# A gated linear recurrence and a ReGLU layer in one kernel: steps 0 and 1 regrouped from two batches of 128 tokens a unit to one batch of 256

## The chip, the cores and the metric

The kernel runs on one core of a Trainium2 chip. The metric is the device time of one execution in microseconds; the figure compared is the median of several executions. The profile and the trace are of one execution, whose own time is given beside its span.

## What is computed

```python
B, H, S, D = 4, 8, 768, 48                    # q, k, v, f_logit: [B, H, S, D], float32
f = 1.0 / (1.0 + np.exp(-f_logit))
for t in range(S):
    state = f[:, :, t, :, None] * state + np.einsum('bhd,bhe->bhde', k[:, :, t], v[:, :, t])
    y[:, :, t] = np.einsum('bhd,bhde->bhe', q[:, :, t], state)
x = y.transpose(0, 2, 1, 3).reshape(B * S, H * D)          # 3072 x 384
out = (np.maximum(x @ w_gate, 0) * (x @ w_val)) @ w_out    # weights 384x1536, 384x1536, 1536x384
```

The kernel works in bf16 inside; inputs and outputs are float32.

## The kernel before

**Chunks and steps.** The recurrence is cut into chunks of 128 tokens. Step c (0 to 5) handles chunk c of all four batches, 512 tokens, and then the feed-forward layer of those 512 tokens. Inside a chunk the recurrence becomes matmuls: the logarithm of the gates is summed over tokens (cum, L567 and L568, or L715), its exponentials scale k and q ("hats", L579 and L583, or L737 and L740), the hats are transposed so that the head dimension lies on partitions (qkT), k times q gives scores (L618 or L780), a causal mask multiplies them (ptm, L623 or L785), and scores times v (intra, L646 or L807) plus q times the state at the chunk's start (inter, L636, the first rounds of L807, or L813) gives x. The state is k hats times v (L684 or L841) added to the old state and scaled by the chunk's decay (L540, L544, L546).

**Duos, in steps 0 and 1.** `attention_duo` takes two batches at once. Batch 2·pr lies on partitions 0 to 63 and batch 2·pr+1 on 64 to 127, and each partition holds two neighbouring tokens, so that a row in memory is 384 bytes long. `load_duo` issues two transfers for each of f, k, q and v, one for each half of the partitions (L454). Even and odd tokens are handled as i = 0 and 1; `tokens` reads them back interleaved, so that x comes out in the order of the tokens. Step 0 has no state to start from, so its inter part is left out, and its state work is planned late (priority P + 30).

**Steps 2 to 5.** `attention_front` and `attention` take one batch and 128 tokens at a time, one token a partition, rows of 192 bytes (loads L466). The hats are transposed in one of two ways: on PE (L751) with a copy by DVE (L756) where the step is in `pe_hats`, which is step 2, otherwise by a transposing DMA that SP issues (L759). In steps 3 to 5 x goes through a transposing DMA too (L832).

**Feed-forward.** `ffn_hidden` makes a block of 128 hidden units: three matmuls with wg (L865), relu on ACT (L871), three with wv (L865), the product on DVE (L875). The first blocks of steps 0 and 1 are made for two batches at a time (256 columns), the others for four (512 columns). `ffn_out` multiplies by wo (L888), ACT copies the result (L898), SP stores it (L902), 192 KB a batch.

**Loads and weights.** The list `first` gives the order of the first loads and weight pieces. SP issues the loads. POOL issues the weights (L486), which are cast from float32 to bf16 on the way, in three pieces each of wg, wv and wo. "wg0@q0.1" means that wg0 is issued only after the load q0.1 has landed. Later loads wait for the landing of the load three before them (`flight`).

**The order of the work.** A planner (`Plan.listed`) sets the order ahead of time: each operation has an assumed length, the operations that it depends on and a priority, and at each step the planner takes the operation that can start first; among equals the lowest priority number goes first. Feed-forward matmuls have 1000 added, so attention goes ahead of them where both are ready. Each engine then runs its list strictly in order, with waits where an operation needs another engine's. The planner also models the two kinds of DMA (`Rings`). PE starts with filler matmuls on zeros (L936, L945) in the gaps that the planner expects before 17 us. Work on PE, DVE, ACT, POOL and SP's DMA issues is all placed this way, so that a changed length or priority can move the rest.

## Time and profile before

| what | value |
|---|---|
| median of 3 runs | 213.52 us (213.44 to 215.12) |
| the profiled execution's own time | 214.66 us |
| its span, first to last instruction | 212.9 us |
| mean granted clock of TensorE | 0.984 of full speed |
| busy: PE, DVE, ACT, POOL | 193.7, 108.6, 108.7, 81.5 us |
| feed-forward matmuls, busy: L865, L888 | 119.9 (wv 61.1, wg 58.8) and 51.3 us |
| DMA | 31.76 MB, mean 149 GB/s |
| first L865 matmul that waits for wv | 24.05 us |
| last load of step 5 issued | 141.2 us |

"Busy" of PE counts pipelined matmuls by modelled ends, so a busy PE is not a PE at its peak; start-to-start distances are the better length of a matmul. In the lines of the timeline the bracket at the end gives the idle time of the engine before the instruction and what ended it. SPq and POOLq stand for the queues that issue DMAs. A wait is put down to the releaser that came last.

### The profile page before, as it was taken

To read this page: it belongs to the slowest core of one execution; us is meant where nothing else is said; L and a number is where in the kernel's file an instruction comes from. 1 tells how busy PE (TensorE), PEld (TensorE's weight loads), DVE (VectorE), ACT (ScalarE), POOL (GpSimd) and SP (SyncE) were. 2 spreads that over 40 slices of the span, in tenths; PEclk is the share of its full clock that TensorE was granted. 3 is DMA by queue.
4 is the path that set the end of the run, shared out by engine and by line. 5 is a ranking of instruction groups with operands and counts; after the bars stand their busy time and mean duration, and the time that the engine had idled before them with its cause. 6 is when DMAs were issued, how large, how long until landed. Compare 5 with 4: busy or idle time off the path is not lost.

```text
span 212.9 us, 4759 instructions
## 1 busy us (share of the span) xinstructions
PE 193.7 (91%) x1929; PEld 109.7 (51%) x1949; DVE 108.6 (51%) x184; ACT 108.7 (51%) x235; POOL 81.5 (38%) x121
## 2 busy tenths in 40 slices
PE   7788599999998999997878999688999999999994
PEld 2265375466776764553433555253555444445562
DVE  7975564582189795664534473253533333233310
ACT  2663167444885878784372654644243344433411
POOL 8939217431795957774515453044000000000000
PEclk9999799999999999999996999999999999999999
DMA  5999999995899899996898995899222100011012
GB/s 125 242 236 220 225 205 220 216 237 121 178 237 210 179 188 189 167 226 133 191 183 183 203 221 125 150 223 150 61 50 64 37 37 37 37 39 38 37 39 109
DMA packets 108069, 31.76 MB, mean 149 GB/s; under 512 B 101136, under 2 KB 108048, under 8 KB 108048
## 3 DMA queue, kind: packets, MB, share of 16 engines
q1 hardware_dynamic: 104064, 27.93, 62.4%
q0 software_dynamic: 3984, 3.54, 10.1%
q8 instruction: 15, 0.25, 0.5%
q14 instruction: 6, 0.05, 0.1%
HBM read 25.95 MB, written 4.72 MB: 144 GB/s over the span
## 4 chain that ended last, share of the span: by engine, by line
PE 66%; DMA 18%; SPq 8%; ACT 2%; POOL 2%; issue 2%; DVE 1%
PE ps L865 37%; PE ps L888 18%; DMA qkT<-hats 5%; DMA wv<-in_moe_w_val_dram 4%; SPq L454 3%; DMA xT<-xn 3%; SPq L832 2%; DMA q_in<-in_q_dram 2%; SPq L759 2%; DMA k_in<-in_k_dram 2%; DMA f_in<-in_f_logit_dram 2%; PE ps L780 2%; PE ps L618 1%; PE ps L715 1%; PE ps L646 1%
## 5 line engine op out<-in xcount | busy, mean ns | idle before, releaser
L875 DVE TENSOR_TENSOR gT<-relu,ps 128x512 bf16<-128x512 bf16 (+1 forms) x82 | 50.2, 620 | 57.9 <-PE ps L865 51.1
L871 ACT ACTIVATE relu<-ps 128x512 bf16<-128x512 f32 (+1 forms) x82 | 44.5, 545 | 37.5 <-PE ps L865 34.3
L865 PE MATMUL ps<-xT,wv 128*128 128x512 bf16 (+1 forms) x243 | 61.1, 361 | 2.3 <-DMA wv<-in_moe_w_val_dram 2.2
L865 PE MATMUL ps<-xT,wg 128*128 128x512 bf16 (+1 forms) x231 | 58.8, 360 | 1.4 <-DMA wg<-in_moe_w_gate_dram 0.4
L888 PE MATMUL ps<-wo,gT 128*128 128x384 bf16 x288 | 51.3, 326 | 0.0
L888 PEld LDWEIGHTS ps<-wo,gT 128*128 128x128 bf16 x288 | 27.1, 98 | 19.2 <-issue 0.2
L865 PEld LDWEIGHTS ps<-xT,wv 128*128 128x128 bf16 x246 | 23.5, 100 | 24.0 <-DMA wv<-in_moe_w_val_dram 2.5
L865 PEld LDWEIGHTS ps<-xT,wg 128*128 128x128 bf16 x246 | 23.1, 100 | 20.4 <-issue 0.8
L898 ACT ACTIVATE osb<-ps 128x384 f32<-128x384 f32 x24 | 11.7, 489 | 34.3 <-PE ps L888 34.2
L785 DVE TENSOR_TENSOR ptm<-ps,tri 128x512 bf16<-128x512 f32 x32 | 21.0, 686 | 13.6 <-PE ps L780 13.5
L737 POOL TENSOR_TENSOR hats<-k_in,expo 128x384 bf16<-128x384 f32 x16 | 15.9, 999 | 22.3 <-DMA k_in<-in_k_dram 14.8
L546 POOL TENSOR_TENSOR st<-ssum,dec 128x384 bf16<-128x384 f32 x16 | 13.2, 828 | 14.1 <-DVE ssum L544 14.1
L740 POOL TENSOR_TENSOR hats<-q_in,expo 128x384 bf16<-128x384 f32 x16 | 15.9, 997 | 4.1 <-DMA q_in<-in_q_dram 4.1
L780 PE MATMUL ps<-qkT 48*128 48x128 bf16 x128 | 6.4, 219 | 6.9 <-DMA qkT<-hats 6.9
L544 DVE TENSOR_TENSOR ssum<-ps,st 128x384 f32<-128x384 f32 x16 | 8.8, 553 | 4.9 <-PE ps L841 4.7
L623 DVE TENSOR_TENSOR ptm<-ps,seen 128x512 bf16<-128x512 f32 x16 | 10.1, 685 | 2.2 <-PE ps L618 2.2
L605 DVE COPY qkT<-ps 128x1024 bf16<-128x1024 bf16 x7 | 4.8, 691 | 10.8 <-PE ps L598 10.7
L945 PE MATMUL ps<-zeros 128*128 128x512 bf16 x30 | 10.0, 481 | 0.1
L706 ACT ACTIVATE f_in<-f_in 128x768 f32<-128x768 f32 x8 | 6.7, 840 | 6.3 <-DMA f_in<-in_f_logit_dram 6.3
L772 POOL CAST vpad<-v_in 128x384 bf16<-128x384 f32 x16 | 7.9, 504 | 4.7 <-DMA v_in<-in_v_dram 4.6
L780 PEld LDWEIGHTS ps<-qkT 48*128 48x128 bf16 x128 | 3.6, 94 | 11.8 <-DMA qkT<-hats 9.5
L725 ACT ACTIVATE expo<-ps 128x384 f32<-128x384 f32 x16 | 7.9, 493 | 2.6 <-PE ps L718 2.5
(90 smaller groups left out, 182.1 us busy)
## 6 DMA issues: line engine op xcount, KB each, us to landing
out_dram<-osb SPq DMA_DIRECT2D x24, 192.0 KB, 2.2
f_in<-in_f_logit_dram SPq DMA_DIRECT2D x8, 384.0 KB, 4.7
k_in<-in_k_dram SPq DMA_DIRECT2D x8, 384.0 KB, 4.5
q_in<-in_q_dram SPq DMA_DIRECT2D x8, 384.0 KB, 5.5
v_in<-in_v_dram SPq DMA_DIRECT2D x8, 384.0 KB, 5.8
f_in<-in_f_logit_dram SPq DMA_DIRECT2D x8, 192.0 KB, 5.0
k_in<-in_k_dram SPq DMA_DIRECT2D x8, 192.0 KB, 6.5
q_in<-in_q_dram SPq DMA_DIRECT2D x8, 192.0 KB, 6.3
```

Of the source, the lines that this page charges most:

```text
L546: add("POOL", lambda: gp.tensor_tensor(t4(s_new), t4(tmp), rate, ALU.mult), [key] + dk, [f"S{b}_{c % 2}"], prio=P + 8, **pool_t(HD))
L623: last_mask[0] = add("DVE", lambda i=i, j=j, s=sj[j]: ve.tensor_tensor(ptm_all[:, m0 + i, j, :, :], s.ap[:, :].rearrange("p (n t) -> p n t ...
L737: add("POOL", lambda: gp.tensor_tensor(hk, kin[:, b % 2, :, :], ex[:, 1, :].rearrange("p (h d) -> p h d", h=H), ALU.mult), in_keys("k", c, ...
L740: add("POOL", lambda: gp.tensor_tensor(hq, qin[:, b % 2, :, :], ex[:, 0, :].rearrange("p (h d) -> p h d", h=H), ALU.mult), in_keys("q", c, ...
L780: mm = te.matmul(s.ap[:, p * C:(p + 1) * C], tokens(c, b, 1, p, lo, lo + D), tokens(c, b, 0, p, lo, lo + D))
L785: add("DVE", lambda j=j, s=s: ve.tensor_tensor(ptm[mi][:, j, :, :], s.ap[:, :].rearrange("p (n t) -> p n t", n=NP), mask, ALU.mult), [s, " ...
L865: mm = te.matmul(bank.ap[:, 0:n], wt[:, kt, j * 128:(j + 1) * 128], xT[xi][:, kt, n0:n1], start=(kt == 0), stop=(kt == NK - 1))
L871: add("ACT", lambda: sc.activation(relu[ri][:, 0:n], gate.ap[:, 0:n], AF.Relu), [gate], [f"relu{ri}"], prio=P, **act_t(n))
L875: add("DVE", lambda: ve.tensor_tensor(gT[gi][:, j, n0:n1], relu[ri][:, 0:n], val.ap[:, 0:n], ALU.mult), [val, f"relu{ri}"], [f"gT{gi}_{j}_ ...
L888: mm = te.matmul(o[b].ap[:, 0:DM], gT[gi][:, j, b * C:(b + 1) * C], wo[:, j, :], start=(j == 0), stop=(j == NJ - 1))
L898: add("ACT", lambda b=b, oi=oi: sc.activation(osb[oi][:, :], o[b].ap[:, 0:DM], AF.Copy), [o[b]], [f"osb{oi}"], prio=P, **act_t(DM))
L945: return te.matmul(spare[:, 0:WARM], zeros[:, 0:128], zeros[:, 0:WARM], start=True, stop=True, skip_group_check=True)
```

## The change

The first two steps are handled in units of one batch and 256 tokens. Unit b takes chunks 0 and 1 of batch b; units 0 and 1 give the 512 tokens of the first feed-forward step, units 2 and 3 those of the second. One transfer fills all 128 partitions, two neighbouring tokens a partition as before, so that partitions 0 to 63 hold chunk 0 and 64 to 127 hold chunk 1. The scores, the masks and x stay in the order even tokens, odd tokens, and only the store puts the rows back in place. Chunk 1 needs the state after chunk 0 of the same unit, so the decay, the state and its scaling come ahead of the scores in each unit, and an inter part follows the intra part of chunk 1. The split of a few products and copies among DVE, ACT and POOL changes. Step 2's hats are transposed by DMA like those of steps 3 to 5. The list of loads and weights has a new order and other anchors.

```diff
-    duos = (0, 1)
-    pe_hats = {2}
+    units = (0, 1)
+    pe_hats = set()
...
-    first = ("f0.0 k0.0 q0.0 f0.1 k0.1 q0.1 v0.0 v0.1 wg0@q0.1 wv0 wg1@v0.1 wv1 wg2 wv2 f1.0 k1.0 q1.0 v1.0 "
-             "wo0@k1.0 wo1@q1.0 wo2 f1.1 k1.1 q1.1 v1.1").split()
+    first = ("f0 k0 v0 q0 f1 k1 q1 v1 wg0@k1 wv0 wg1 wv1 wg2 wv2 f2 k2 q2 v2 wo0@k2 wo1 wo2@v2 f3 k3 q3 v3").split()
...
+    def load_unit(n, b, after=()):
         t = ld[n]
         row = NL[n] * 2 * HD
...
+        c, pr = b // 2, b % 2
+        src = bass.AP(tensor=srcs[n].tensor, offset=b * H * S * D, ap=[[2 * D, 128], [S * D, H], [1, 2 * D]])
+        dst = bass.AP(tensor=t, offset=slot_of(n, c, pr) * 2 * HD, ap=[[row, 128], [2 * D, H], [1, 2 * D]])
...
+        op = add("SP", lambda: sy.dma_start(dst, src), [], in_keys(n, c, 2 * pr, 2 * pr + 2), occ=0.45, lat=1.5,
+                 prio=b * 10, after=after, follows=[last] if last else [])
...
+    def tokens2(q0, u, x, p, lo=0, hi=128, only=None):
         row = NQ * 2 * NP * C
...
-        return bass.AP(tensor=qkT, offset=at, ap=[[row, hi - lo], [1, 64], [C, 2]])
+        return bass.AP(tensor=qkT, offset=at, ap=[[row, hi - lo], [C, 2], [1, 64]])
...
+    def attention_unit(b):
+        w0, P = 2 * b, (0, 6, 40, 60)[b]
+        late = b > 1
...
-            ke = "POOL" if c or (pr and i) else "DVE"
-            qe = "DVE" if c == 0 and i == 0 else "POOL"
+            ke = "POOL" if late else "DVE"
+            qe = "DVE" if not late and i == 0 else "POOL"
...
-                key["v"] + [f"vpad{vi}"], [f"v_{vi}"], prio=P + 5, **pool_c(HD))
+                key["v"] + [f"vpad{vi}"], [f"v_{vi}"], prio=P + 2, **pool_c(HD))
...
-            e = "ACT" if c == 0 and pr and x else "DVE"
-            add(e, (lambda tp=tp, x=x: sc.activation(qk2(q0, x), tp.ap[:, :].bitcast(BF16), AF.Copy)) if e == "ACT"
...
+            add("DVE", lambda tp=tp, x=x: ve.tensor_copy(qk2(q0, x), tp.ap[:, :].bitcast(BF16)),
...
-              kv, occ=0.36, lat=PE_L, prio=P + (30 if c == 0 else 6), opens=kv)
...
+              kv, occ=0.45, lat=PE_L, prio=P + 4, opens=kv)
+        dk = [f"decu_{b}{j}" for j in range(2)]
+        new_state(kv[0], 0, b, w0, P, decu[:, b, 0, :, :], dk)
...
+        def inter():
+            for n, (p, i) in enumerate(blocks):
+                lo = 32 * (n % 4)
+                mm = te.matmul(ys[1].ap[lo:lo + 32, n // 4 * C:(n // 4 + 1) * C],
+                               st[b][0][:, p * SSTEP + 32 * i:p * SSTEP + 32 * i + 32], tokens2(q0, 1, 0, p),
+                               start=False, stop=(n >= 8), skip_group_check=True)
+            return mm
...
+        chain("inter", "PE", inter, both + [f"S{b}_0", ys[1]], [ys[1]], occ=0.25, lat=PE_L, prio=P + 7)
...
+        new_state(kv[1], 1, b, w0 + 1, P + (4 if late else 30), decu[:, b, 1, :, :], dk)
...
+            if g in units:
+                at = ((2 * g + b // 2) * S + b % 2 * C) * DM
+                to = bass.AP(tensor=out.tensor, offset=at, ap=[[DM, 2], [2 * DM, 64], [1, DM]])
```

## The prediction

> **What bounds the kernel.** I read the page first, then the table of windows in one-microsecond stretches at the start and in ten-microsecond stretches after it, then the chain of waits, the timeline round two stages, and SP's own queue.

> ```profile
> PE 193.7 (91%) x1929; PEld 109.7 (51%) x1949; DVE 108.6 (51%) x184; ACT 108.7 (51%) x235; POOL 81.5 (38%) x121
> ```

> TensorE is busy for 91% of the span, so the question is where the other 19 us lie. By the windows 6 lie before 25 us (with 10 us of filler matmuls, L945, beside them), 8.4 between 95 and 150 us, 3 at the end. The start, by the chain of waits:

> ```profile
> 8.50 5.16 DMA q_in<-in_q_dram
> ...
> 13.97 0.93 POOL wg L486
> 14.89 9.12 DMA wv<-in_moe_w_val_dram
> 24.05 3.34 PE ps L865 x15
> ```

> The sixth load lands at 13.97, lets POOL issue the first weights, and the first value weights land at 24.05. The first x was ready at 20.81 (end of the two L657 copies): the weights end last, not the attention. The windows show what the wait leaves behind:

> ```profile
> 13.00:14.00 1.00, 1.00 (x16) 0.72 (x19) 0.64 (x1) 0.51 (x2) 0.03 (x1) 1.00 1.30 240
> ...
> 22.00:23.00 1.00, 0.00 (x0) 0.00 (x0) 1.00 (x3) 0.26 (x1) 0.57 (x2) 1.00 1.16 288
> ...
> 25.00:26.00 1.00, 1.00 (x7) 0.67 (x5) 0.30 (x1) 0.38 (x1) 0.00 (x0) 0.50 1.19 212
> ```

> The last three columns are granted clock, DMA share and GB/s. The DMA moves 230 to 250 GB/s from 3 us on; PE is idle at 22 to 24 and then runs at a clock of 0.5 until 27. From there to 95 us it hardly waits:

> ```profile
> 60.00:70.00 10.00, 9.33 (x224) 7.11 (x222) 8.42 (x19) 6.79 (x18) 7.75 (x10) 1.00 1.02 214
> 70.00:80.00 10.00, 9.68 (x152) 6.75 (x152) 8.99 (x17) 7.97 (x23) 7.31 (x10) 1.00 0.93 186
> ```

> So in step 2's stage a microsecond off PE is a microsecond off the end, provided that nothing new is waited for.

> **Step 2's transposes leave PE.** The timeline has them in pairs with a DVE copy:

> ```profile
> 75.15 0.61 PE L751 MATMUL ps<-ident,hats 128*128 128x128 bf16 x8
> 76.14 0.68 DVE L756 COPY qkT<-ps 128x1024 bf16<-128x1024 bf16 x1
> ```

> The chain gives 0.45 us for eight of them; four batches: **-1.8**. The copies (4 x 0.68) cost nothing now and bring nothing: DVE is at 84 to 90% beside a PE at 93 to 97%, and the one wait of PE for DVE here (L636 on ptm, 0.67) is the most they could return.

> **In their place come four crossings on SP.** The nearest rows are steps 3 to 5:

> ```profile
> qkT<-hats SPq DMA_TRANSPOSE x12, 4.4
> ...
> 102.17 0.40 PE L780 MATMUL ps<-qkT 48*128 48x128 bf16 x8 [0.42 <-DMA qkT<-hats]
> ...
> 136.36 0.40 PE L780 MATMUL ps<-qkT 48*128 48x128 bf16 x8 [1.44 <-DMA qkT<-hats]
> ```

> Step 3's four crossings made PE wait 0.42 in all, step 5's 3.90 (1.44, 1.21, 1.25, 0). Step 2 resembles step 3: feed-forward work of the step before is at hand. But step 2's x is also wanted soon. Batch 3's q hats end at 73.45 and qkT is copied at 76.82, 3.4 us; an unblocked issue (1.3) and landing (4.4) take 5.7, 2.3 more. Step 2's last x (81.17 + 0.49 = 81.66) has 4.15 us until its first use (85.81), and with PE some 2.7 earlier only 1.4: a stall of 0.9. Ends: +0.4 and +3.9; I take **+0.9**.

> [...] This trace has 0.45 us for eight on PE and 4.4 to land for eight by DMA.

> **What is queued behind them.** SP takes its work in order, and in this stage its issues take 1.4 us and more, where a free one takes 0.43 (the load at 45.0):

> ```profile
> 75.91 1.66 SPq L466 DMA_DIRECT2D k_in<-in_k_dram  x1
> 77.74 1.42 SPq L466 DMA_DIRECT2D q_in<-in_q_dram  x1
> 79.43 1.75 SPq L466 DMA_DIRECT2D v_in<-in_v_dram  x1
> 81.23 3.66 SPq L759 DMA_TRANSPOSE qkT<-hats  x1
> ```

> Four crossings at 1.3 put 5.2 us ahead of step 3's last loads, and SP waits for hats besides. That v already came late (POOL's cast at 85.70 waited 1.72). What covers it is 60 us of feed-forward work that PE has in hand at 150 us; the cover is gone where PE's written order puts scores ahead of it, as it did for much of the 8.4 us after 95. Ends: -1 (the new order falls better) and +5.2; I take **+0.5**, nearest to step 3, whose loads were as late.

> **Attention work moves ahead of 24 us.** The state matmuls (L684, 0.45 for a pair) of the second unit and the first unit's share of inter (half of L636's 0.86 to 0.93) now fit into the idle time before the weights. Before, one set of state matmuls and all of inter came later. Ends 0 and -0.9; I take **-0.9**, since 2.2 us stand empty there. Over steps 0 and 1 the counts of matmuls, masks and copies stay. One k product moves from POOL to DVE (1.00 to 0.56 us), a qkT copy from ACT and an x copy from DVE change places; all finish under the weights' wait, and would cost 0.6 to 0.7 each without it.

> **The loads.** wg0 still hangs on the sixth load (k1 where it was q0.1). The six are 2.36 MB. SP's issues fall from two of 0.61 to 0.78 us to one a load, but SP was not the limit: at 9.27 six loads were issued and four moved. Does one transfer on 128 partitions run faster than two on 64? No row shows it. The nearest for 128 partitions (L466, pieces of 192 bytes) is 237 GB/s on the page, so no gain; the fastest microsecond shown, 288 GB/s, would bring the sixth load and with it 24.05 forward by 2.36/0.242 - 2.36/0.288 = 1.6. I take the middle, **-0.8**.

> [...]

> **POOL's order.** Weights beyond the first pair have priority 6. The second duo's products stood at 4, ahead of them; the second unit's stand at 8, behind. Four issues of 0.78 go ahead of its q product (17.11 before; about 13.9 + 6 x 0.78 = 18.6 now), then scores about 21 and x near 26 to 29 (28.7 before). The first unit's feed-forward covers up to there (seven groups of three matmuls, 0.64 each at half clock, from 24.05 to 28.5); it is longer only by the new chain state, scaled state, inter. Also wo2 waits for v2 on POOL, in front of v casts that need v2 anyway: 0.78, covered by PE's 44 to 50 us of other work. Ends: 0 (covered) and +2.2 (the masks and the intra matmuls after the first group instead of before); I take **+0.6**. The third and fourth units wait for nothing new that PE has not other work for; stores keep 1536-byte rows, 0.

> **Sum.** -1.8 + 0.9 + 0.5 - 0.9 - 0.8 + 0.6 = -1.5 on the span of 212.9, that is 211.4, and 213.2 for that execution of 214.66. The median, 213.52, is 1.1 below it; my forecast for a median is 213.5 - 1.5 = **212.0**, own range 210 to 213.6.

> **Rivals.** (1) *The loads do gain from 128 partitions* and the planner's new order falls better by 1 us after 95: all favourable ends, -1.8 + 0.4 - 1 - 0.9 - 1.6 + 0 = -4.9 at most, 208.6; with half of the better order 209.1. For: the DMA is the first stage's limit. Against: halves already overlap. (2) *Crossings starve PE*: the row for step 5 decides in step 2, +3.9, and the loads behind SP's waits +4; with -1.8 and -0.9 that is +5.2, 218; at half of both, 214.7; about 216.5. It decides from the point where a crossing issued in step 2 lands over 6 us after its hats, since the slack is 4.15. For: DMA at 1.02 share here, issues held for 2 to 3.7 us. Against: step 3's 0.42. (3) *The second unit comes late*: its scores are written behind the first value matmul, which waits until 24; then scores (1.2), four masks (2.5) and intra (0.8) follow that, less the 2.3 that the first group covers: +2.2, and up to +3 with the clock at 0.5, in place of 0.6: 213.6 to 214.4. For: the margin between hats q at 19.6 and the weights. Against: PE serves attention first when both are ready. (4) *The change does not issue the first weights later*, whatever its words: wg0 follows the sixth load before and after. Then the start stays and -0.8 falls away: 212.8, within the forecast.

> **Chances.** Forecast 0.40, rival 1 0.20, rival 2 0.28, rival 3 0.12. About 1% is what a measurement of this kernel can tell from no change. Faster by over 1% (under 211.4): 0.4 of the forecast and rival 1, together 0.36. Slower by over 1% (over 215.7): most of rival 2 and part of 3, 0.31, and 0.04 for both together with a worse order later: 0.35. Between: 0.29. The range takes in rival 1 and most of rival 2: 207.5 to 218.5.

> **What would show it.** First L865 matmul on wv at 23.0 to 24.1; no L751 or L756; L780's waits in step 2 under 1.5 us; PE over 9.5 of 10 from 30 to 80; idle PE from 95 to 150 between 7 and 10 us. Wrong if the first value weights land outside 22 to 25, or if SP holds a load for over 4 us in step 2.

## The result and the profile after

The changed kernel takes **232.81 us** (median of 4 runs, 231.0 to 234.49) against 213.48 for the kernel before in the same comparison: a ratio of 1.087, 95% interval 1.076 to 1.098. The forecast was 212.0 with a range of 207.5 to 218.5, so both the size and the sign are wrong. Ratios leave out the executions that took over 1.5% more than the fastest of their kernel; medians keep them. The profiled execution took 232.29, with a span of 230.5 and a mean granted clock of 0.933.

First the page of the kernel after: its span, the busy time of each engine, and GB/s in 40 slices of 5.8 us.

```profile
span 230.5 us, 4706 instructions
...
PE 199.3 (86%) x1918; PEld 109.8 (48%) x1918; DVE 109.5 (47%) x182; ACT 108.4 (47%) x235; POOL 82.2 (36%) x120
...
GB/s 184 325 268 207 206 205 211 228 201 126 83 115 77 220 210 195 171 160 123 107 158 120 180 194 75 181 216 118 215 146 69 51 37 34 34 33 29 32 46 102
```

PE was 19.2 us short of a busy span before and is 31.2 us short now (230.5 - 199.3). These 12.0 us are new idle time; the other 5.6 of the 17.6 us by which the span grew are busy time, although fewer PE records are listed. The windows show where that comes from; the columns are the length, then busy time and instructions of PE, PEld, DVE, ACT and POOL, then granted clock, DMA share and GB/s:

```profile
5.00:10.00 5.00, 4.54 (x24) 1.89 (x22) 4.82 (x8) 3.45 (x9) 5.00 (x10) 1.00 1.17 324
...
60.00:70.00 10.00, 7.32 (x62) 5.48 (x61) 4.10 (x9) 4.24 (x14) 4.41 (x6) 0.76 0.78 109
70.00:80.00 10.00, 5.46 (x59) 3.65 (x57) 2.68 (x6) 2.62 (x9) 1.95 (x3) 0.55 1.11 147
```

The start has gained: 324 GB/s between 5 and 10 us, where the kernel before moved 242. The loss is between 60 and 80 us, where the prediction had expected PE to be busy more than 9.5 us of 10: 7.32 and 5.46 are left, at a clock of 0.76 and 0.55, and the traffic is 109 and 147 GB/s where it was 214 and 186. Single microseconds inside that stretch, and just ahead of it, look like this:

```profile
57.00:58.00 1.00, 1.00 (x14) 0.85 (x11) 1.00 (x3) 0.95 (x4) 1.00 (x2) 1.00 0.13 49
...
60.00:61.00 1.00, 1.00 (x15) 0.85 (x14) 0.00 (x0) 1.00 (x4) 0.59 (x2) 1.00 0.13 49
...
73.00:74.00 1.00, 0.00 (x0) 0.00 (x0) 0.00 (x0) 0.00 (x0) 0.00 (x0) 0.50 0.13 49
```

Look at the two columns at the end. A DMA share of 0.13 is 2/16, the packet time of two of the core's sixteen DMA engines, and they move 49 GB/s. In the trace's packet records at 57 and 60 us the stores' rows are nearly all that moves, about two at a time. At 73 us every compute engine stands still meanwhile: 19 packets of a crossing (a transposing transfer qkT<-hats) that began between 69.2 and 70.5 us end together at 74.4, just behind the stores' last packet at 74.2. What SP had issued just before (start, time SP spent on the issue, instruction):

```profile
51.05 1.63 SPq L895 DMA_DIRECT2D out_dram<-osb  x2
52.72 0.77 SPq L467 DMA_DIRECT2D k_in<-in_k_dram  x1
53.53 7.93 SPq L467 DMA_DIRECT2D q_in<-in_q_dram  x1
61.51 2.33 SPq L748 DMA_TRANSPOSE qkT<-hats  x1
63.89 1.08 SPq L895 DMA_DIRECT2D out_dram<-osb  x2
65.02 5.84 SPq L748 DMA_TRANSPOSE qkT<-hats  x1
```

The pattern repeats: two stores (L895), and then the second or even the first issue behind them takes 6 to 8 us. Two stores of 197 KB at 49 GB/s would take 8.0 us (2 x 197/49); the packets of the first two run from 52.34 to 61.32, and q_in is held up for 7.93. The chain of waits puts both on the path (start, length, step), and PE's timeline shows who waited, with the idle time and its releaser in brackets:

```profile
53.53 11.29 DMA q_in<-in_q_dram
...
65.02 10.68 DMA qkT<-hats
```

```profile
65.86 0.61 PE L769 MATMUL ps<-qkT 48*128 48x128 bf16 x8 [2.68 <-DMA qkT<-hats]
...
75.83 0.61 PE L769 MATMUL ps<-qkT 48*128 48x128 bf16 x8 [4.54 <-DMA qkT<-hats]
```

The trap is in the last two fences. Chain, waits and timeline all name the crossings (qkT<-hats) and the loads, that is, the transfers that came late. They do not name the store that they stood behind, because nothing waits for a store. Only SP's queue and the DMA share point to it.

### The profile page after: what moved, and what is told of

Read it like the earlier page. It is cut to its first block, busy times and chain, and to the rows that moved or that the text cites. A ratio compares the mean times of both kernels' runs of the same rounds, so it can differ in the third digit from the quotient of the medians.

```text
span 230.5 us, 4706 instructions
## 1 busy us (share of the span) xinstructions
PE 199.3 (86%) x1918; PEld 109.8 (48%) x1918; DVE 109.5 (47%) x182; ACT 108.4 (47%) x235; POOL 82.2 (36%) x120
## 4 chain that ended last, share of the span: by engine, by line
PE 60%; DMA 20%; SPq 7%; ACT 5%; DVE 4%; issue 1%; POOL 1%; DVEq 0%; POOLq 0%
PE ps L854 32%; PE ps L877 15%; DMA qkT<-hats 11%; DMA q_in<-in_q_dram 7%; SPq L467 3%; PE ps L938 3%; SPq L748 2%; DMA f_in<-in_f_logit_dram 2%; PE ps L769 2%; DVE hats L574 2%; DVE ptm L646 2%; PE ps L608 2%; ACT relu L860 1%; SPq L895 1%; POOL hats L729 1%
## 5 line engine op out<-in xcount | busy, mean ns | idle before, releaser
L854 PE MATMUL ps<-xT,wg 128*128 128x512 bf16 (+1 forms) x246 | 64.4, 374 | 0.0
L854 PE MATMUL ps<-xT,wv 128*128 128x512 bf16 (+1 forms) x246 | 64.1, 372 | 0.0
L877 PE MATMUL ps<-wo,gT 128*128 128x384 bf16 x288 | 53.3, 332 | 0.0
L854 PEld LDWEIGHTS ps<-xT,wv 128*128 128x128 bf16 x246 | 24.2, 104 | 21.3 <-issue 1.9
L854 PEld LDWEIGHTS ps<-xT,wg 128*128 128x128 bf16 x246 | 23.8, 103 | 20.7 <-issue 1.6
L887 ACT ACTIVATE osb<-ps 128x384 f32<-128x384 f32 x24 | 11.8, 490 | 34.4 <-PE ps L877 34.3
L769 PE MATMUL ps<-qkT 48*128 48x128 bf16 x128 | 7.5, 247 | 19.4 <-DMA qkT<-hats 19.3
L769 PEld LDWEIGHTS ps<-qkT 48*128 48x128 bf16 x128 | 4.3, 106 | 26.4 <-DMA qkT<-hats 16.7
L543 POOL TENSOR_TENSOR st<-ssum,dec 128x384 bf16<-128x384 f32 x12 | 9.9, 830 | 10.6 <-DVE ssum L541 10.6
L938 PE MATMUL ps<-zeros 128*128 128x512 bf16 x33 | 10.5, 472 | 0.0
L613 DVE COPY qkT<-ps 128x1024 bf16<-128x1024 bf16 x8 | 5.5, 687 | 7.0 <-PE ps L608 7.0
## 6 DMA issues: line engine op xcount, KB each, us to landing
wv<-in_moe_w_val_dram POOLq DMA_DIRECT2D x3, 384.0 KB, 13.9
```

The lines of the kernel that those rows point to most:

```text
L543: add("POOL", lambda: gp.tensor_tensor(t4(s_new), t4(tmp), rate, ALU.mult), [key] + dk, [f"S{b}_{c % 2}"], prio=P + 8, **pool_t(HD))
L769: mm = te.matmul(s.ap[:, p * C:(p + 1) * C], tokens(c, b, 1, p, lo, lo + D), tokens(c, b, 0, p, lo, lo + D))
L854: mm = te.matmul(bank.ap[:, 0:n], wt[:, kt, j * 128:(j + 1) * 128], xT[xi][:, kt, n0:n1], start=(kt == 0), stop=(kt == NK - 1))
L877: mm = te.matmul(o[b].ap[:, 0:DM], gT[gi][:, j, b * C:(b + 1) * C], wo[:, j, :], start=(j == 0), stop=(j == NJ - 1))
L887: add("ACT", lambda b=b, oi=oi: sc.activation(osb[oi][:, :], o[b].ap[:, 0:DM], AF.Copy), [o[b]], [f"osb{oi}"], prio=P, **act_t(DM))
L938: return te.matmul(spare[:, 0:WARM], zeros[:, 0:128], zeros[:, 0:WARM], start=True, stop=True, skip_group_check=True)
```

## The experiments

**The first theory (A).** The store of steps 0 and 1 writes its rows back in order through the destination pattern `[[DM, 2], [2 * DM, 64], [1, DM]]`. Its slowest dimension is 2, and only two DMA engines take part (the share of 0.13). What SP issues next waits for these two, so loads and crossings land late (q_in after 11.29 us, a crossing after 10.68). That the wait is for these two was my estimate, from the crossing's 19 packets that end at 74.4, just behind the stores' last. **Its rivals:** the four crossings themselves hold SP's queue (the prediction's rival 2); rows written out of order are slow as such; the new units cost something in the order of the work.

Ratios are to the kernel before, run beside the experiments on the same chip; its medians there were 212.88 (e1 to e4), 213.12 (e5 to e8) and 212.55 (e9 to e12), on three chips.

### e1: the same store as two transfers of 64 rows

```diff
-                to = bass.AP(tensor=out.tensor, offset=at, ap=[[DM, 2], [2 * DM, 64], [1, DM]])
...
-            both = [(to, osb[oi][:, :])]
+                both = [(bass.AP(tensor=out.tensor, offset=at + i * DM, ap=[[2 * DM, 64], [1, DM]]), osb[oi][64 * i:64 * i + 64, :])
+                        for i in range(2)]
...
```

> The changed kernel with each store of steps 0 and 1 issued as two transfers of 64 rows instead of one whose pattern begins with a dimension of 2; every engine's order is the same otherwise. Theory A (the store is moved by two of sixteen DMA engines, at 49 GB/s, and what SP issues behind it lands late): 209 to 214 us, no stretch with 40 to 55 GB/s between 50 and 140 us, PE over 9 of 10 from 60 to 80, L769's waits in step 2 under 1.5 us in all. Theory B (the crossings of step 2 starve PE by themselves): 226 to 233 us, the waits of 2.7 and 4.5 us on qkT stay. Theory C (the planned order and the late second unit cost it): 228 to 233 us.

Measured: **214.17 us**, ratio 1.0081 (1.0033 to 1.0129); 18.6 of the 19.3 us are gone, though the time is 0.2 us above the range of theory A. The same rows go to the same scattered places, now as two transfers whose first dimension is 64. The planner's length for the issue is left as it was, so that the written order stays. SP's queue, with four issues for two stores, and the windows:

```profile
52.58 2.46 SPq L895 DMA_DIRECT2D out_dram<-osb  x4
55.09 0.59 SPq L467 DMA_DIRECT2D k_in<-in_k_dram  x1
55.72 1.63 SPq L467 DMA_DIRECT2D q_in<-in_q_dram  x1
```

```profile
60.00:70.00 10.00, 9.57 (x194) 7.61 (x192) 6.69 (x16) 7.75 (x23) 6.97 (x9) 1.00 1.18 157
70.00:80.00 10.00, 8.69 (x119) 4.63 (x121) 6.55 (x13) 7.16 (x18) 5.05 (x7) 1.00 1.13 207
```

The issue of q_in behind the stores takes 1.63 us where it took 7.93, and PE is busy for 18.3 of the 20 us where it was 12.8 (8.69 in the second stretch is under the 9 expected). The crossings are all still there, and PE waits 1.38 us for those of step 2 (0.43 and 0.95). DVE, ACT and POOL run the same lists as in the changed kernel, so the order of the work is not the cause either.

### e2: the kernel before, with only the store's pattern

```diff
-            both = [(bass.AP(tensor=out.tensor, offset=at, ap=[[DM, C], [1, DM]]), osb[oi][:, :])]
+            rows = [[DM, 2], [2 * DM, 64]] if g in duos else [[DM, C]]
+            both = [(bass.AP(tensor=out.tensor, offset=at, ap=rows + [[1, DM]]), osb[oi][:, :])]
```

> The kernel before with the store pattern of the change in steps 0 and 1 (dimensions 2, 64, 384) and nothing else; the rows of those steps come out in the wrong order. Theory A: 220 to 230 us, stretches of 49 GB/s after 50 us, out of step 0's and step 1's stores. Theories B and C: 213 to 215 us, since transfer sizes and rows are the same.

Measured: **239.23 us**, ratio 1.122 (1.1146 to 1.1294). The pattern alone, in a kernel with no other part of the change, costs 26 us, 9 more than theory A's range allowed. The same two signs appear, in SP's queue and in the windows:

```profile
50.58 5.87 SPq L903 DMA_DIRECT2D out_dram<-osb  x1
...
57.22 5.37 SPq L466 DMA_DIRECT2D v_in<-in_v_dram  x1
```

```profile
61.00:62.00 1.00, 1.00 (x14) 0.90 (x11) 0.88 (x2) 0.67 (x2) 0.14 (x1) 1.00 0.13 49
```

### e3 and e4: step 2's transposes back on TensorE, without and with the split store

```diff
-    pe_hats = set()
+    pe_hats = {2}
```

> The changed kernel with step 2's transposes back on PE (pe_hats = {2}), its store kept. Theory A: 220 to 231 us, since loads still queue behind the stores; the stretches of 49 GB/s stay, and waits move from qkT to loads. Theory B: 211 to 215 us.

> Both: two-transfer stores and step 2's transposes on PE. Theory A: 210 to 214 us; beside the run with the two-transfer store alone it prices the crossings: by my terms of the prediction (-1.8 for PE's transposes, +0.9 and +0.5 for waits) it should be 0.4 us slower than that run. Theory B: the same as the run with only the transposes on PE, 211 to 215.

Measured: e3 (the changed store kept) **232.11 us**, ratio 1.0882 (1.0806 to 1.0957), no different from the change itself and 1 us above theory A's range. e4 (e1 and this edit) **212.86 us**, ratio 0.9967 (0.9922 to 1.0011). So rival 2 falls as the cause of the loss: with step 2's crossings gone and the store kept, all of the loss stays. e3 less e4, which differ in the store alone and were run side by side, puts the store's price at 19.3 us.

Once the store is out of the way, e4 is below e1, by 1.3 us by the medians and 1.1% by the ratios (2.4 us), and the two intervals just miss each other. The traces do not show that the crossings are the reason. PE waits 1.38 us for them in e1, less than the 1.8 that the transposes take in e4 (4 x 0.45; one runs from 63.08 to the next matmul at 63.53); and e4's profiled execution leads by 3.2 us at the first block of 512 columns (30.94 against 34.09), before step 2, and by 1.8 at the end (spans 210.6 and 212.4).

### e6 and e7: the dose

The kernel before once more, with the same store in groups of 4 and of 16:

```diff
-            both = [(bass.AP(tensor=out.tensor, offset=at, ap=[[DM, C], [1, DM]]), osb[oi][:, :])]
+            rows = [[DM, 4], [4 * DM, 32]] if g in duos else [[DM, C]]        # e6
+            rows = [[DM, 16], [16 * DM, 8]] if g in duos else [[DM, C]]       # e7
+            both = [(bass.AP(tensor=out.tensor, offset=at, ap=rows + [[1, DM]]), osb[oi][:, :])]
```

> The kernel before with the stores of steps 0 and 1 as patterns of dimensions 4, 32, 384 (rows of those steps come out in another order). Theory A, if the leading dimension sets how many engines move the store: a store of 197 KB goes at about 98 GB/s, takes 2 us in place of 4, and the time lies between 217 and 226 us. Rival (rows that are not neighbours in memory are slow, whatever the leading dimension): the same as the pattern 2, 64, 384, 236 to 240 us.

> The kernel before with the stores of steps 0 and 1 as patterns of dimensions 16, 8, 384 (rows in another order). Theory A: all sixteen engines move it, 212 to 215 us, no different from before. Rival (scattered rows are slow): 230 to 240 us.

Measured: e6 **225.11 us**, ratio 1.0571 (1.0511 to 1.063); e7 **212.76 us**, ratio 1.0004 (0.9968 to 1.004). A leading dimension of 2, 4 and 16 costs 26, 12 and 0 us for rows that are out of order each time. This rules out scattered rows as the cause. A window and an issue of e6, a quarter of the engines (0.25 = 4/16), 78 GB/s and a held-up store:

```profile
58.00:59.00 1.00, 1.00 (x30) 0.86 (x23) 1.00 (x2) 0.52 (x2) 0.00 (x0) 1.00 0.25 78
```

```profile
51.19 3.70 SPq L903 DMA_DIRECT2D out_dram<-osb  x1
```

In e7 the same issue took 1.47 us, and no microsecond from 51 to 66 us has a share under 0.47. So a first dimension of 2 stood at 0.13 and 49 GB/s, and one of 4 at 0.25 and 78 GB/s, which fits one engine for each of its entries; with 16 the share does not tell the store from what moves beside it. The traces do not tell which engine moved a packet, but two stores issued together still show 0.13, not 0.25, which fits the same two.

### e5: the first loads in halves again

e1, with each load of steps 0 and 1 as two transfers to 64 partitions each, the planner's list unchanged:

```diff
-        dst = bass.AP(tensor=t, offset=slot_of(n, c, pr) * 2 * HD, ap=[[row, 128], [2 * D, H], [1, 2 * D]])
+        ops = [(bass.AP(tensor=t, offset=64 * x * row + slot_of(n, c, pr) * 2 * HD, ap=[[row, 64], [2 * D, H], [1, 2 * D]]),
+                bass.AP(tensor=srcs[n].tensor, offset=b * H * S * D + 128 * x * D, ap=[[2 * D, 64], [S * D, H], [1, 2 * D]]))
+               for x in range(2)]
...
```

> The run e1_store_two with every load of steps 0 and 1 issued as two transfers on 64 partitions each, and every engine's order the same otherwise. Theory L (the loads run faster because one transfer fills all 128 partitions): 232 to 249 GB/s from 5 to 15 us in place of 317 to 324, wg0 issued near 13.7 in place of 11.8, and 1 to 3 us slower than e1_store_two. Rival (the speed of the loads comes from their order or from fewer issues): 310 GB/s or more, wg0 near 12, the same time as e1_store_two within 1 us.

Measured: **219.91 us**, ratio 1.0311 (1.0252 to 1.037): 5.7 us above e1 by the medians, 2.3% by the ratios, more than the 1 to 3 expected. The window that moved 324 GB/s in the kernel after, and the wait that is back:

```profile
5.00:10.00 5.00, 4.38 (x24) 1.64 (x22) 4.82 (x8) 3.55 (x8) 5.00 (x10) 1.00 1.19 237
```

```profile
23.97 0.82 PE L855 MATMUL ps<-xT,wv 128*128 128x256 bf16 x3 [1.62 <-DMA wv<-in_moe_w_val_dram]
```

One transfer on 128 partitions ran faster here than two on 64 (324 against 237 GB/s at nearly the same DMA share, 1.17 and 1.19), which no row of the trace of before had shown.

The 5.7 us are not the price of that speed alone. By the profiles e5 is level with e1 at the ninth feed-forward product on DVE (gT, 35.4 us in both) and 4.5 us behind at the seventeenth (64.7 against 60.2). What lies between is one late load: SP's issues for these loads are doubled, the second half of v2 is issued at 23.75 us where e1 issued v2 at 12.78, with weights moving in between, and it lands at 41.06 where e1's landed at 29.86. POOL waits for it before it issues wo2, and PE waits for the hats behind that:

```profile
41.36 0.80 POOL L488 DMA_DIRECT2D wo<-in_moe_w_out_dram  x1 [5.15 <-DMA v_in<-in_v_dram]
```

```profile
43.24 0.62 PE L609 MATMUL ps<-ident,hats 128*128 128x128 bf16 x8 [2.78 <-POOL hats L575]
```

How much of this is the doubled issues and how much the speed was not separated.

### e8, e10, e11: does the start decide?

By its profile e4 begins its 512-column blocks at 30.94, 2 us before the kernel before (32.97), and yet its time is the same. Three edits of e4: the second unit's second k product on POOL (e8), wg0 behind f1 in place of k1 (e10), the planner's time for a first load 1.21 in place of 1.41 (e11).

```diff
-            ke = "POOL" if late else "DVE"
+            ke = "POOL" if late or (b and i) else "DVE"                       # e8
-    first = ("f0 k0 v0 q0 f1 k1 q1 v1 wg0@k1 ...
+    first = ("f0 k0 v0 q0 f1 k1 q1 v1 wg0@f1 ...                              # e10
-        dma(op, f"{n}{slot_of(n, c, pr)}", 1.41, 1, 1024)
+        dma(op, f"{n}{slot_of(n, c, pr)}", 1.21, 1, 1024)                     # e11
```

> The run e4_two_pe_hats with the second unit's odd k product on POOL instead of DVE. What is left of the start is then the theory: PE waits 2.2 us at 18.3 for that product (1.65 us on DVE beside POOL's casts) and feed-forward stands behind it, at 21.87. Without it feed-forward starts near 20.3 unless the weights end last, then at 21 to 22; the time 0.5 to 1.5 us under e4_two_pe_hats, 211.3 to 212.5, if the gain lasts. Rival (what the start gains is given back in the waits after 90 us, whose sum was 10 us there against 8.4 before): no change, 212.5 to 213.5.

> The kernel with two-part stores and TensorE transposes in step 2, with the first gate weights issued behind the fifth load (f1) where they were behind the sixth (k1). If the weights bound the start, the 512-column blocks begin about 1 us earlier than 30.9 and the time is 0.5 to 1 lower, 212.0. If the attention's products bound it (the first feed-forward matmul waited for a hats copy on VectorE and not for weights), the start stays at 30.9 and the time within 0.5 of 212.9; the second unit then comes later and it may be 0.5 slower.

> The kernel with two-part stores and TensorE transposes in step 2, with the planner's time for a first-steps load set from 1.41 to 1.21 us, the 393 KB at the 324 GB/s that the profile showed. Only the written order of the engines can change. If the order after 80 us is what gives the start's 2 us back, another order moves that: 211 to 212.5. If the gain is lost to what the transfers and engines do whatever the order, 212.9 within 0.5.

Measured: e8 **214.08**, ratio 1.0032 (0.9989 to 1.0075); e10 **213.58**, 1.0015 (0.9962 to 1.0067); e11 **214.27**, 1.0048 (1.0008 to 1.0088). None gains. In e8 PE's pause for the second unit's k hats fell from 2.15 to 1.73 us, but PE then waits 0.49 for the q hats, so nothing was won there. e10 tells nothing on the weights: POOL issued wg0 at 11.76 us as in e4 (11.77), right behind a cast and a product in its written order, so the other anchor did not move it. e11 put the engines in another order and lost, so a better order was not to be had in this way.

Beside these, the profiles of the whole set show something that none of the edits aimed at. PE waits for the first hats until 11.0 us (11.2 in the kernel before and its variants), by an amount that differs from one profile to the next though PE's list up to there is the same in the changed kernel and all runs built on it (one filler of e11 is not in its trace). Timeline of e1, then of e4:

```profile
11.02 0.80 PE L608 MATMUL ps<-ident,hats 128*128 128x128 bf16 x8 [2.35 <-DVE hats L574]
```

```profile
11.03 0.62 PE L608 MATMUL ps<-ident,hats 128*128 128x128 bf16 x8 [1.95 <-DVE hats L574]
```

In e1 the granted clock then falls to 0.5, in e4 it does not. Windows of e1:

```profile
11.00:12.00 1.00, 0.98 (x16) 0.79 (x18) 1.00 (x1) 0.00 (x0) 1.00 (x2) 0.66 1.17 326
12.00:13.00 1.00, 0.67 (x17) 0.58 (x13) 1.00 (x3) 0.00 (x0) 1.00 (x2) 0.50 1.17 325
13.00:14.00 1.00, 1.00 (x9) 0.91 (x9) 0.30 (x1) 0.00 (x0) 1.00 (x2) 0.50 1.17 324
```

Over all profiles, those that paused 1.50 to 1.95 us here (the change, e4, e5, e8, e10 and the kernels with the start of before) kept the full clock, and those that paused 2.14 to 2.35 (e1, e3, e9, e11, e12) lost it for 3.41 us. The length of the pause is not what decided here, though. In the traces' clock records every change lies a whole number of stretches of 3.41 us behind the first rise to full speed, and that rise comes between 4.25 and 7.25 us, differently in each profile. In e1 it came at 4.49, so the fillers ran faster and ended earlier (8.67 us), and the pause lay within one stretch: of the 3.41 us from 7.90 on PE was idle for 2.35, and the clock was halved at 11.31. In e4 it came at 6.31, the fillers ended at 9.07, and two stretches shared the pause, with 0.65 and 1.59 us idle: the clock stayed.

The first 512-column block began at 30.9 to 32.7 in the change, e4, e8 and e10, at 33.8 in e5, whose weights came late, and at 32.5 to 34.3 where the clock fell here. The profiled execution of e4 has a mean clock of 0.992, and of its ten executions only one other reaches 0.99; the rest have 0.967 to 0.984. So its median probably lacks the start that the profile shows, but those executions have no trace. Nor does the start decide alone: e12, whose clock fell, has the shorter span, 209.9 us against e4's 210.6. A kernel with more filler ahead of 11 us was not run.

### e9 and e12: transposes on TensorE in later steps as well

```diff
-    pe_hats = {2}
+    pe_hats = {2, 3}        # e9
+    pe_hats = {2, 5}        # e12
```

> The kernel with two-part stores and TensorE transposes in step 2, with step 3's four batches of hats turned by TensorE as well. If crossings cost PE time wherever the feed-forward work does not cover them (step 2's cost 1.3 us net of the 1.8 that the transposes take), and step 3's are dearer now that the start is earlier, 211.5 to 212.5 against 212.9. If step 3's crossings are covered, as they were in the kernel before (PE waited 0.42 us for all four), the 32 transposes are added to a busy PE: +1.5 to +1.8, 214.4 to 214.7.

> The kernel with two-part stores and TensorE transposes in step 2, with step 5's four batches of hats turned by TensorE as well. Its worst single wait was PE for a crossing of a late step, 3.49 us at 131.87. If that wait goes and nothing takes its place, -3.5 + 1.8 for the transposes, 211.2. If hats or loads are late there whatever turns them, PE waits for the hats in place of the crossing and pays the 1.8: 213.5 to 214.7.

Measured: e9 **213.22**, ratio 1.0084 (1.0028 to 1.0139); e12 **213.01**, 1.0015 (0.9964 to 1.0067). Against e4, which ran beside another set of the kernel before, e9 is 1.2% slower by the ratios (2.5 us) but 0.3% by the medians (0.7 us). The traces do not show that step 3's transposes cost it: e9's profiled execution is 3.4 us behind e4's at the first 512-column block (34.31), long before step 3, and 2.4 behind at the end. So whether step 3's crossings are covered stays open. In step 5 nothing is gained: e4's wait of 3.49 us for a crossing at 131.87 is gone, but PE now waits for the hats themselves:

```profile
136.29 0.62 PE L740 MATMUL ps<-ident,hats 128*128 128x128 bf16 x8 [1.39 <-POOL hats L729]
```

e12's time lies between what was expected of the two theories, so it does not decide between them. No run beats the kernel before by more than a measurement of it can tell; the best, e4, has an interval up to 1.0011.

## Why the prediction was wrong

**The step that failed** is the clause at the end of the part on POOL's order: "stores keep 1536-byte rows, 0". I judged the store by the length of its rows and by its bytes. Both are as before. What had changed was the order of the dimensions in the destination, from 128 rows to 2 groups of 64, and with it the number of engines. The diff that I quoted shows it (`ap=[[DM, 2], [2 * DM, 64], [1, DM]]`), and no row of the trace of before has a transfer of that form; the other waits of the sum got ends from both sides, and this one got a zero without any. In its place the runs show a store on 2 of 16 engines at 49 GB/s, SP's next issues held for up to 7.93 us, and 18.6 us lost. No rival contains it either: rival 2 names the stretch where PE starves and the crossing it waits for, but by a mechanism that e3 refutes. (Its own sum, 213.5 + 5.2, is 218.7 and not 218.)

Measured shares of the 19.3 us (232.81 - 213.48), against the sum of -1.5:

| term | predicted | measured | from |
|---|---|---|---|
| the store's pattern | 0 | +18.6 (19.3) | after less e1 (e3 less e4) |
| step 2: PE's transposes out, crossings in, loads behind them | -1.8 + 0.9 + 0.5 = -0.4 | +1.3 (2.4 by the ratios) | e1 less e4 |
| attention earlier, loads, POOL's order | -0.9 - 0.8 + 0.6 = -1.1 | -0.7 (-1.7 to +0.2); 0.0 by the medians | e4's ratio times 212.9 |

- **The crossings: forecast -0.4, measured +1.3, and not settled.** The measured difference has the other sign and lies inside the ends given (-1.8 + 0.4 - 1 = -2.4 to -1.8 + 3.9 + 5.2 = +7.3), but PE's waits for step 2's crossings in e1, 1.38 us against the 0.9 forecast, are still less than the 1.8 that the transposes take. In which waits the difference lies was not separated. In step 2 the medians are against the crossings by 1.3 us; in step 3 e9, with the transposes on PE, is the slower, by 0.7 to 2.5 us that its trace does not place. I had also left out step 4 of the kernel before, whose waits for crossings come to 2.57 us (0.34 and 2.23), between the two steps that I took as ends.
- **Loads: the size was off.** I took -0.8 of at most -1.6 and argued that halves overlap already. The 324 GB/s are beyond the 288 that I had as the fastest row, the first gate weights are issued at 11.79 in place of 13.97, and the first value weights land at 22.38 in place of 24.01, the whole 1.6. With halves in the new schedule e5 is 5.7 us slower, much of it behind one late load.
- **The first value matmul landed in its window for another reason.** It runs at 23.25, inside the 23.0 to 24.1 forecast, but it waits for no weight. The attention's hats end last: PE pauses 2.16 us until 20.45 for the second unit's hats, and one k product on DVE takes 1.65 us there, where its neighbours take 0.85 and 1.04. So of the 1.6 us by which the value weights come earlier 0.8 showed, and "the weights end last" no longer holds.
- **Rival 4** was right that the weights are not issued later; they are issued 2.2 us earlier.
- **The signs of failure were well chosen.** "SP holds a load for over 4 us in step 2" was met by 7.93 (and a crossing was held for 5.84), "PE over 9.5 of 10 from 30 to 80" failed at 60, the waits on qkT in step 2 came to 7.2 us (2.68 and 4.54) where under 1.5 was forecast, and PE was idle for 12.0 us between 95 and 150 where it was 7 to 10. They point to SP's queue, which is where the cause was found.

What stays open: why the pattern costs 26 us in the kernel before and 18.6 to 19.3 in the changed one, what step 2's and step 3's crossings cost against transposes on PE, and where the 5.7 us of e5 would have gone had the planner been told of the halves.

## What to carry to other kernels

When a diff touches an access pattern, read its dimensions from the slowest on, not only its bytes and its rows: a first dimension of 2 put a 197-KB store on 2 of 16 engines at 49 GB/s, and the same rows as two transfers with a first dimension of 64 cost nothing that e4 shows. A slow store that nobody waited for still sat on the path through what its queue issued next (q_in, held for 7.93 us); a DMA share that stood at 0.13 or 0.25, with SP's issues held for 3.7 to 8 us, was its mark here, while the chain and the waits named only its victims.

## What the runs showed of the hardware beyond that

```profile
4.61 1.85 DVE L410 COPY seen<-later 64x128 bf16<-64x128 bf16 x1
...
6.92 2.48 DVE L410 COPY seen<-later 64x128 bf16<-64x128 bf16 x1
9.41 0.80 DVE L574 TENSOR_TENSOR hats<-k_in,expo 128x384 bf16<-128x384 f32 x1
```

These are of the kernel after, where a qkT copy of sixteen times the elements takes 0.69 us. POOL is busy for all of 5 to 10 us, mostly with memsets; whether they are the reason was not tried.
